# The first tokens by GpSimd's queue, the first weights on two queues: a start-up change in a gated mix of sliding attention and MLP

## The chip, the cores and the metric

One core of a Trainium2 chip runs one program. The metric is the device time in microseconds (us); lower is better. The times of the kernel before are three runs, and one further execution was profiled.

## The reference

For 2048 tokens of width 448, two branches are mixed by a gate of the token itself:

```python
g = sigmoid((x * gate_w).sum(-1, keepdims=True))
a = A(x, wqkv, wo)            # 16 heads of 28; each token attends to itself and 7 earlier ones, 2 apart
b = relu(x @ w1 + b1) ** 2 @ w2 + b2      # 448 -> 1792 -> 448
return g * a + (1 - g) * b
```

All inputs and the output are float32. In branch A, `qkv = x @ wqkv`, the eight logits of a token are scaled, masked where the position would be negative, put through a softmax, applied to the values, and multiplied by `wo`.

## The kernel before, in words

**Products in three parts.** Every operand of a matmul is kept as a high part, rounded to the chip's fp32r type, and a low part, the raw value less the high one. A product is three matmuls: high by high, high by low, low by high. So each raw tile that arrives is rounded by ScalarE (`activation(..., AF.Copy)` into an fp32r tile) and subtracted by VectorE (`tensor_sub`), and only then can all three matmuls run.

**Tiles.** The tokens are four chunks of 512, each transposed in four tiles of rows of the 448: three of 128 and one of 64, which stands twice, on both halves of the partitions. `x.h[k]` and `x.l[k]` are the high and low parts of tile k of a chunk, `x.x7` and `x.x8` those of the last. The first block of weights (queries, 448 columns and two for the gate) is `wqh`/`wql` for k = 0, 1, 2 and `w7h`/`w7l` for the last tile. Raw data land in `raws[0]` (weights, "wqraw" in the profile) and `rx` (tokens, "xraw").

**Stages.** TensorE makes q, k, v of the four chunks, which go to DRAM and come back with their halos; then attention is multiplied out on GpSimd and reduced on VectorE while TensorE does the MLP over the chunks (`ORDER`), ending with the products by `wo` and the mix.

**Order.** A planner (`Plan`) decides at build time, from costs in ns and its own clock `plan.t`, in which order jobs are put on ScalarE, VectorE, GpSimd and SyncE's DMA queue. It starts only after the opening, at `START`; the opening is written out by hand. `WARM` empty matmuls on zeros come first on TensorE (L807, "warm"). Then `qkv_first` (L429) makes the queries of chunk 0: for k = 0 it takes the first two of four token groups (columns 0 to 255, the first half) through all three products, two matmuls each, and then the other two; for k = 1 and 2 all four together. From L341 on, products run as pairs on the two halves of TensorE's rows.

**The opening's data.** ScalarE's queue brings `rx[:, 0]` in two halves of columns (L813). SyncE's queue brings the weights and the tokens of k = 1, 2 and 3 by turns (L816, L819, L821), then the other weights of chunk 0. Eight semaphores go round over the DMAs of both queues, so the ninth waits for the first to land. For k = 0, ScalarE rounds the weights (L831) and the second half of the tokens (L834), VectorE rounds the first half (L836) and makes the low parts of weights (L838) and tokens (L839). At the top, before anything else, GpSimd clears the mask (L239, L241) and a tile of zeros for the halos (L306).

Of the kernel before, what the change touches and what calls it, by code (L numbers as in the profile page):

```python
# [9 lines left out]
AF = mybir.ActivationFunctionType  # L10
# [4 lines left out]
P = 128  # L15
NS = 8
HALO = W - 1
# [6 lines left out]
NQ = D + 2  # L24
# [7 lines left out]
MM448, MM512 = 189.2, 216.0  # L32
PE_LAT = 175.0
LAT = 60.0
START = 4900.0
ORDER = (3, 0, 1, 2)
WARM = 19
FIRST = (2700.0, 2350.0, 2300.0)
PP_BUFS = 4
ST_BUFS = 3  # L40
# [143 lines left out]
def gated_mix_kernel(ctx: ExitStack, tc: tile.TileContext, xT, wqkv, w1, w2, wo, b1, b2, out):  # L184
    nc = tc.nc

    def f32(ap):
        return ap.bitcast(F32)
# [35 lines left out]
    mask = const.tile([P, NS, W], F32, name="mask")  # L224
# [11 lines left out]
    b1z = biasp.tile([P, 16], F32, name="b1z")  # L236
    b1t, none = b1z[:, :NF], b1z[0:1, 15:16]
    ctx.enter_context(tc.manual_schedule())
    nc.gpsimd.memset(mask, 0.0)  # L239
    for s in range(HALO):  # L240
        nc.gpsimd.memset(mask[0:1, s, 0:HALO - s], -1e9)  # L241

# [35 lines left out]
    def x_slot(j, o=16):  # L280
        return x_place[0][:, o + 2 * CH * j:o + 2 * CH * (j + 1)].rearrange("p (i n) -> p i n", i=2)

    def x_tiles(c):
        if c % 2:
            x_place[0] = xpool.tile([P, 8 * CH + 16], F32R, tag="x", name=f"x{c}")
            return [x_slot(j, 0 if c == 1 else 16) for j in range(4)]
        return [xap.tile([P, 2, CH], F32R, tag=f"x{j}", name=f"x{c}_{j}") for j in range(4)]
# [11 lines left out]
    wqh = ap.tile([P, 3, NP + 2 * D], F32R, name="wqh")  # L299
    wql = ap.tile([P, 3, NP + 2 * D], F32R, name="wql")  # L300
# [2 lines left out]
    ap.tile([P, 48], F32, name="pad_a")  # L303

    halo0 = smp.tile([2 * G * HALO, C], F32, tag="lg", name="halo0")
    nc.gpsimd.memset(halo0, 0.0)  # L306

    stage = {}
    stores = {(d, par): [] for d in range(3) for par in range(2)}
# [495 lines left out]

    for _ in range(WARM):
        nc.tensor.matmul(warm[:, :2 * P].rearrange("p (i n) -> p i n", i=2), zero, zeros, start=True, stop=True)  # L807

    raws = [rawp.tile([P, 4, 512], F32, tag="raw", name="wqraw0")]
    rx = rawp.tile([P, 4, 512], F32, tag="raw", name="xraw0")  # L810
    halves = slice(0, 256), slice(256, CH)
    for cols in halves:
        nc.scalar.dma_start(rx[:, 0, cols], xT[0, :, 0, cols])  # L813
    for k in range(4):
        if k < 3:
            nc.sync.dma_start(raws[0][:, k, :NQ], wqkv[0, :, k])  # L816
        else:
            for b, rows in ((0, slice(0, 64)), (1, slice(64, P))):
                nc.sync.dma_start(raws[0][rows, k, :NQ], wqkv[b, rows, k])  # L819
        if k:  # L820
            nc.sync.dma_start(rx[:, k], xT[0, :, k])  # L821
# [4 lines left out]
        raws.append(raw)  # L826
    raw7 = attp.tile([P, D], F32, tag="q", name="wqraw7")
    nc.sync.dma_start(raw7, wqkv[2, :, 3, :D])
    x = X(x_tiles(0))
    for k in range(3):  # L830
        nc.scalar.activation(wqh[:, k, :NQ], raws[0][:, k, :NQ], AF.Copy)  # L831
        for n, cols in enumerate(halves if k == 0 else (slice(0, CH),)):
            if k or n:
                nc.scalar.activation(x.h[k][:, cols], rx[:, k, cols], AF.Copy)  # L834
            else:
                nc.vector.tensor_copy(x.h[k][:, cols], rx[:, k, cols])  # L836
            if not n:
                nc.vector.tensor_sub(wql[:, k, :NQ], raws[0][:, k, :NQ], f32(wqh[:, k, :NQ]))  # L838
            nc.vector.tensor_sub(x.l[k][:, cols], rx[:, k, cols], f32(x.h[k][:, cols]))  # L839
    nc.scalar.activation(w7h[:, :NQ], raws[0][:, 3, :NQ], AF.Copy)  # L840
    nc.vector.tensor_sub(w7l[:, :NQ], raws[0][:, 3, :NQ], f32(w7h[:, :NQ]))
# [3 lines left out]

    plan.t, plan.wire = START, 15000.0
    plan.now = 9800.0
# [64 lines left out]
    for c in range(4):  # L912
        x = xs[c]
# [305 lines left out]
    rows = wo_d.rearrange("(i b) n -> i b n", b=14)  # L1219
# [31 lines left out]
    for g in range(2, 2 * NF):  # L1251
# [5 lines left out]
        if not f:  # L1257
            x, slots = X([nxt[j][0] for j in range(4)]), [nxt[j][1] for j in range(4)]
# [105 lines left out]
```

## Time and profile before

| | |
|---|---|
| timed runs, median (lowest to highest) | 393.45 us (393.07 to 393.51), 3 runs |
| the profiled execution's own time | 392.84 us |
| its span, first to last instruction | 391.1 us |
| TensorE busy in the span | 386.5 us, 99% |
| VectorE, ScalarE, GpSimd busy | 260.3, 205.4, 260.6 us |
| moved by DMA | 73.75 MB, mean 189 GB/s |

Times inside the profile count from the first instruction of the span. An engine's busy time says nothing of whether what it does is needed: the empty matmuls of the opening count as busy too. A bracket behind a row of the timeline, such as `[1.27 <-DMA wqraw<-wqkv]`, is the time for which the engine stood idle before it and what ended that. PEld is TensorE's loading of the stationary operand, which overlaps the matmul before it.

### The profile page before, as it was taken

How to read it: one execution, taken by the hardware profiler on the slowest of the kernel's cores; microseconds unless marked ns; L12 is line 12 of the kernel's file. 1: busy time of each engine (PE TensorE's matmuls, PEld its weight loads, DVE VectorE, ACT ScalarE, POOL GpSimd, SP SyncE). 2: the span in 40 equal slices, each digit the busy share in tenths (PEclk: the TensorE clock that was granted, in tenths of full speed). 3: DMA queues.
4: the chain of work that ended last, by engine and by line, in shares of the span. 5: the costliest groups of instructions: out<-in, count | busy, mean ns of one | idle time of the engine just before them, and what ended most of it. 6: DMA issues, size and time to landing. Idle time of an engine off the chain costs nothing.

```text
span 391.1 us, 9273 instructions
## 1 busy us (share of the span) xinstructions
PE 386.5 (99%) x3829; PEld 385.3 (99%) x3829; DVE 260.3 (67%) x346; ACT 205.4 (53%) x501; POOL 260.6 (67%) x165
## 2 busy tenths in 40 slices
PE   9999999999999999999999999999999999999996
PEld 8999999999999999999999999999999999999995
DVE  4525523588585778778656989789666686668454
ACT  5857865362566566445555445345716343456740
POOL 0000003979999989959999887999998979661000
PEclk9999999999999999999999999999999999999999
DMA  7999999997174062644203779645635220226835
GB/s 240 399 356 318 373 369 355 377 340 267 49 253 151 1 219 80 220 167 164 90 2 137 244 209 271 218 112 141 217 106 166 84 96 2 88 64 164 141 106 189
DMA packets 64697, 73.75 MB, mean 189 GB/s; under 512 B 32336, under 2 KB 57488, under 8 KB 64272
## 3 DMA queue, kind: packets, MB, share of 16 engines
q1 hardware_dynamic: 64224, 72.79, 56.4%
q8 instruction: 30, 0.49, 0.5%
q10 hardware_dynamic: 432, 0.38, 0.3%
q14 instruction: 11, 0.09, 0.1%
HBM read 45.71 MB, written 28.25 MB: 189 GB/s over the span
## 4 chain that ended last, share of the span: by engine, by line
PE 99%; DVE 0%; DVEq 0%; issue 0%
PE b L341 33%; PE h L341 32%; PE qkv L341 23%; PE a L341 7%; PE qkv L429 2%; PE warm L807 1%; PE a L1154 1%; DVE bt_b L1037 0%; DVEq L1359 0%
## 5 line engine op out<-in xcount | busy, mean ns | idle before, releaser
L539 POOL TENSOR_TENSOR pp<-q,k 128x896 f32<-128x896 f32 x56 | 116.8, 2119 | 75.1 <-DMA k<-k_d 63.5
L341 PE MATMUL h<-x,w1h 64*128 64x512 f32 x672 | 122.0, 376 | 0.0
L551 POOL TENSOR_TENSOR pp<-lg,v 128x896 f32<-128x896 f32 x64 | 113.9, 1868 | 9.4 <-DVE o L561 5.0
L341 PE MATMUL qkv<-wqh,x 64*128 64x448 f32 (+1 forms) x528 | 83.2, 350 | 0.0
L341 PEld LDWEIGHTS h<-x,w1h 64*128 64x128 f32 x672 | 82.8, 186 | 0.0
L341 PE MATMUL h<-x,w1l 64*128 64x512 f32 x336 | 75.9, 376 | 0.0
L793 DVE TENSOR_TENSOR h<-h,h 128x512 fp32r<-128x512 f32 x56 | 38.7, 691 | 55.1 <-ACT h L792 54.9
L543 DVE TENSOR_REDUCE lg<-pp 128x32 f32<-128x896 f32 x64 | 66.9, 1076 | 12.5 <-POOL pp L539 12.5
L341 PE MATMUL b<-w2bh,h 64*128 64x448 f32 x448 | 69.5, 349 | 0.0
L341 PE MATMUL b<-w2ah,h 64*128 64x448 f32 x448 | 69.2, 349 | 0.0
L561 DVE TENSOR_REDUCE o<-pp 128x112 f32<-128x896 f32 x64 | 67.5, 1066 | 0.0
L341 PEld LDWEIGHTS qkv<-wqh,x 64*128 64x128 f32 x528 | 61.0, 186 | 0.0
L341 PE MATMUL qkv<-wql,x 64*128 64x448 f32 (+1 forms) x264 | 56.8, 350 | 0.0
L789 ACT ACTIVATE h<-h,b1z 128x512 f32<-128x512 f32 x56 | 36.7, 655 | 37.1 <-PE h L341 37.1
L341 PEld LDWEIGHTS b<-w2bh,h 64*128 64x128 f32 x448 | 53.2, 193 | 0.0
L341 PEld LDWEIGHTS b<-w2ah,h 64*128 64x128 f32 x448 | 53.1, 193 | 0.0
L341 PE MATMUL b<-w2bl,h 64*128 64x448 f32 x224 | 47.6, 349 | 0.0
L341 PE MATMUL b<-w2al,h 64*128 64x448 f32 x224 | 47.5, 349 | 0.0
L341 PEld LDWEIGHTS h<-x,w1l 64*128 64x128 f32 x336 | 44.0, 186 | 0.0
L791 ACT ACTIVATE h<-h 128x512 fp32r<-128x512 f32 x56 | 33.4, 597 | 1.6
L363 ACT ACTIVATE st<-qkv 128x448 f32<-128x448 f32 x48 | 24.3, 539 | 17.8 <-PE qkv L341 11.5
L341 PEld LDWEIGHTS qkv<-wql,x 64*128 64x128 f32 x264 | 33.2, 186 | 0.0
(108 smaller groups left out, 576.4 us busy)
## 6 DMA issues: line engine op xcount, KB each, us to landing
v<-v_d SPq DMA_DIRECT2D x8, 840.0 KB, 6.8
x_d<-x SPq DMA_DIRECT2D x12, 512.0 KB, 7.3
x<-x_d SPq DMA_DIRECT2D x12, 512.0 KB, 4.1
k<-k_d SPq DMA_DIRECT2D x7, 840.0 KB, 7.4
q_d<-st SPq DMA_DIRECT2D x8, 448.0 KB, 5.8
k_d<-st SPq DMA_DIRECT2D x8, 448.0 KB, 5.7
v_d<-st SPq DMA_DIRECT2D x8, 448.0 KB, 6.4
o_d<-o SPq DMA_DIRECT2D x16, 224.0 KB, 2.1
```

Of the source, the lines that this page charges most:

```text
L341: nc.tensor.matmul(woven_out(acc.pt, acc.n), a[rows], woven(w[rows]), start=acc.todo == acc.all, stop=acc.todo == 1)
L363: nc.scalar.activation(st[0][:, :, t % 2].rearrange("p (i g) c -> p i g c", i=2), unwoven(pt[:, :D]).rearrange("p i (g c) -> p i g c", c=C ...
L429: nc.tensor.matmul(woven_out(acc.pt, NQ), a, woven(w), start=k == j == 0, stop=False)
L539: nc.gpsimd.tensor_mul(pr.rearrange("p (w c) -> p w c", w=W), q[:, s:s + 1].to_broadcast([P, W, C]), k[:, s:s + W])
L543: nc.vector.tensor_reduce(lgs[i][:, s], pr.rearrange("p (w h d) -> p w h d", w=W, h=HG), axis=AX.X, op=ALU.add)
L551: nc.gpsimd.tensor_mul(pr.rearrange("p (h d w) -> p w h d", h=HG, w=W), lgs[i][:, s][:, :, :, None].to_broadcast([P, W, HG, DH]), vs[i][:, ...
L561: nc.vector.tensor_reduce(o_t[par, s][:, g * C:(g + 1) * C], pr.rearrange("p (c w) -> p c w", w=W), axis=AX.X, op=ALU.add)
L789: a = add(ACT, 656.0, lambda pt=pt, r=r: nc.scalar.activation(pt, pt, AF.Relu, bias=b1t[:, f + r:f + r + 1]), ready, bias_job[0], prio=NEXT)
L791: b = add(ACT, 600.0, lambda pt=pt, hh=hh: nc.scalar.activation(hh, pt, AF.Square), a, prio=NEXT)
L793: low = add(DVE, 690.0, lambda pt=pt, hh=hh, hl=hl: nc.vector.tensor_sub(hl, pt, f32(hh)), a, prio=NEXT)
L807: nc.tensor.matmul(warm[:, :2 * P].rearrange("p (i n) -> p i n", i=2), zero, zeros, start=True, stop=True)
L1154: nc.tensor.matmul(woven_out(acc.pt, D), a, woven(w), start=False, stop=acc.todo == 1)
```

## The change

The tokens' first half of k = 0 no longer comes raw to be rounded by VectorE: GpSimd's queue brings it from DRAM straight into the fp32r tile `x.h[0][:, :256]`, with a cast on the way. The raw tile is still needed for the low part; ScalarE's queue now brings its 512 columns in one DMA. Ahead of that, the weights of k = 0 come as two DMAs of 64 rows, one on ScalarE's queue and one on SyncE's. ScalarE does a 1x1 copy into a spare place as its first operation, so that its table of functions loads there. GpSimd's memsets move behind its DMA. VectorE's rounding of the first half is gone. TensorE's empty matmuls go from 19 to 17, and the planner's start from 4900 to 4650 ns.

```diff
-START = 4900.0
+START = 4650.0
-WARM = 19
+WARM = 17
...
-    nc.gpsimd.memset(mask, 0.0)
-    for s in range(HALO):
-        nc.gpsimd.memset(mask[0:1, s, 0:HALO - s], -1e9)
...
-    nc.gpsimd.memset(halo0, 0.0)
...
     for _ in range(WARM):
         nc.tensor.matmul(warm[:, :2 * P].rearrange("p (i n) -> p i n", i=2), zero, zeros, start=True, stop=True)
 
+    x = X(x_tiles(0))
+    nc.gpsimd.dma_start(x.h[0][:, :256], xT[0, :, 0, :256])
+    nc.gpsimd.memset(mask, 0.0)
+    for s in range(HALO):
+        nc.gpsimd.memset(mask[0:1, s, 0:HALO - s], -1e9)
+    nc.gpsimd.memset(halo0, 0.0)
     raws = [rawp.tile([P, 4, 512], F32, tag="raw", name="wqraw0")]
     rx = rawp.tile([P, 4, 512], F32, tag="raw", name="xraw0")
     halves = slice(0, 256), slice(256, CH)
-    for cols in halves:
-        nc.scalar.dma_start(rx[:, 0, cols], xT[0, :, 0, cols])
+    for e, rows in ((nc.scalar, slice(64, P)), (nc.sync, slice(0, 64))):
+        e.dma_start(raws[0][rows, 0, :NQ], wqkv[0, rows, 0])
+    nc.scalar.dma_start(rx[:, 0], xT[0, :, 0])
+    nc.scalar.activation(b1z[0:1, 14:15], none, AF.Copy)
     for k in range(4):
+        if k == 0:
+            continue
         if k < 3:
             nc.sync.dma_start(raws[0][:, k, :NQ], wqkv[0, :, k])
...
-    x = X(x_tiles(0))
     for k in range(3):
         nc.scalar.activation(wqh[:, k, :NQ], raws[0][:, k, :NQ], AF.Copy)
+        nc.vector.tensor_sub(wql[:, k, :NQ], raws[0][:, k, :NQ], f32(wqh[:, k, :NQ]))
         for n, cols in enumerate(halves if k == 0 else (slice(0, CH),)):
             if k or n:
                 nc.scalar.activation(x.h[k][:, cols], rx[:, k, cols], AF.Copy)
-            else:
-                nc.vector.tensor_copy(x.h[k][:, cols], rx[:, k, cols])
-            if not n:
-                nc.vector.tensor_sub(wql[:, k, :NQ], raws[0][:, k, :NQ], f32(wqh[:, k, :NQ]))
             nc.vector.tensor_sub(x.l[k][:, cols], rx[:, k, cols], f32(x.h[k][:, cols]))
```

## The prediction

> **What bounds the kernel now.** I read the page first, for the engine that sets the end.
>
> ```profile
> span 391.1 us, 9273 instructions
> PE 386.5 (99%) x3829; PEld 385.3 (99%) x3829; DVE 260.3 (67%) x346; ACT 205.4 (53%) x501; POOL 260.6 (67%) x165
> PE 99%; DVE 0%; DVEq 0%; issue 0%
> ```
>
> Busy shares are of the span; the third line is the chain of waits by engine. TensorE (PE) is the chain. So the next question is where PE is not yet doing real work. The windows view, for PE alone (stretch, its length, PE's busy time, instructions, clock, DMA share, GB/s):
>
> ```profile
> 0.00:4.97 4.97, 4.18 (x19) 1.00 0.55 160
> 5.82:12.28 6.46, 6.46 (x36) 1.00 1.02 339
> 12.28:98.99 86.71, 86.71 (x915) 1.00 0.97 344
> 98.99:391.10 292.11, 288.28 (x2862) 1.00 0.44 139
> ```
>
> From 5.82 us PE is filled without a break; the 3.8 us missing in the last stretch are the tail behind the last matmul. Whatever moves the first matmuls moves the end by as much, and nothing that the change touches later is on the path while that filling lasts. The change can only act before about 6 us. The timeline there (start, duration, engine, line, what; in brackets the idle time before and who ended it):
>
> ```profile
> 0.74 0.90 ACTq L813 DMA_DIRECT2D xraw<-xT  x2
> 0.75 0.86 SPq L816 DMA_DIRECT2D wqraw<-wqkv  x2
> 0.79 4.39 PE L807 MATMUL warm<-const-float32-0.0 128*128 128x256 f32 x19 [0.79 <-PEq L1356]
> 1.65 0.43 SPq L821 DMA_DIRECT2D xraw<-xT  x1
> 1.67 1.28 ACT L831 ACT_TABLE_LOAD   x1 [1.67 <-PEq L1356]
> 4.22 0.58 ACT L831 ACTIVATE wqh<-wqraw 128x450 fp32r<-128x450 f32 x1 [1.27 <-DMA wqraw<-wqkv]
> 4.40 0.29 DVE L836 CAST x<-xraw 128x256 fp32r<-128x256 f32 x1 [3.54 <-DMA xraw<-xT]
> 4.55 0.33 PEld L807 LDWEIGHTS warm<-const-float32-0.0 128*128 128x128 f32 x1
> 4.84 0.63 DVE L838 TENSOR_TENSOR wql<-wqraw,wqh 128x450 fp32r<-128x450 f32 x1
> 4.86 0.45 PEld L429 LDWEIGHTS qkv<-wqh,x 128*128 128x128 f32 x2
> 4.97 0.69 PE L429 MATMUL qkv<-wqh,x 128*128 128x452 f32 x2
> 5.38 0.42 DVE L839 TENSOR_TENSOR x<-xraw,x 128x256 fp32r<-128x256 f32 x1
> 5.52 0.30 PEld L429 LDWEIGHTS qkv<-wql,x 128*128 128x128 f32 x2 [0.21 <-DVE wql L838]
> 5.52 0.65 PE L429 MATMUL qkv<-wql,x 128*128 128x452 f32 x2
> 5.55 0.42 ACT L834 ACTIVATE x<-xraw 128x256 fp32r<-128x256 f32 x1 [0.75 <-DMA xraw<-xT]
> 5.85 0.34 PEld L429 LDWEIGHTS qkv<-wqh,x 128*128 128x128 f32 x2
> 6.01 0.55 PE L429 MATMUL qkv<-wqh,x 128*128 128x452 f32 x2
> ```
>
> Read it as a ladder. The first weights land at 4.22, are rounded by 4.80, and PE loads at 4.86. The first half of the tokens lands at 4.40 and is rounded by DVE until 4.69. The warm-ups run at one per (4.55 − 0.75)/18 = 0.211 us, so the 19 of them fill PE to about 4.97, just when the first real matmul starts: nothing is lost there. Matmuls 3 and 4 (low part of the weights) are held by DVE, whose subtraction ends at 5.47: load at 5.52, and with a late load the matmul itself starts about 0.11 later, so this costs about 0.13. Matmul 5 wants the low part of the tokens' first half (DVE, 5.38 to 5.80), gets it and starts at 6.01. From then on PE steps evenly.
>
> **The change, part by part.**
>
> *Fewer warm-ups.* Two less bring the earliest start of real work from 4.97 to 4.97 − 2 × 0.211 = 4.55. This is the most that can be won in front: 0.42 us; with the 0.13 of the third matmul, 0.55 us in all, 0.14% of the time.
>
> *First weights as two halves of 64 rows, on ACT's and SP's queues.* Before, SP's queue held the weights first and ACT's the tokens, and both drained together. The DMA view of the stretch up to the weights' landing, and of the one in which ACT's queue has work (packets, MB, share of 16 engines):
>
> ```profile
> DMA packets 435, 0.58 MB, mean 137 GB/s; under 512 B 34, under 2 KB 435, under 8 KB 435
> DMA packets 648, 0.87 MB, mean 256 GB/s; under 512 B 64, under 2 KB 576, under 8 KB 648
> q1 hardware_dynamic: 360, 0.61, 58.9%
> q10 hardware_dynamic: 288, 0.26, 28.0%
> DMA packets 411, 0.70 MB, mean 377 GB/s; under 512 B 49, under 2 KB 227, under 8 KB 411
> ```
>
> The first line is 0 to 4.25 us, the next three are 1.75 to 5.15 us (q1 is SP's queue, q10 ACT's), the last 5.15 to 7 us. Until 4.25 us 0.58 MB had moved, for weights of 0.23 MB. With both queues starting on the weights, 0.23 MB, or 0.36 with all of GpSimd's half, have to move: at 0.58 MB in the 2.5 us since 1.75 that takes 1.0 to 1.6 us, and they land at 2.8 to 3.4. The rounding (0.58) then ends at about 4.0, ahead of 4.55. The weights stop being the last to come; so does their low part, at about 4.65, ahead of matmul 3. Both terms are off the path, and so the 0.13 is won.
>
> A rule of the Trainium skill speaks against this part: DMA: Bandwidth & Descriptors, section Rules for kernel authors, says of two transfers to disjoint halves of the partitions not to bother, since they share the same 16 engines. The row says that the engines are shared by what is queued first; by the rule alone the weights would still land at 4.22 (a rival below).
>
> *The table of functions.* Its load (1.67 to 2.95) already ended 1.27 us before ACT's first data. It moves nothing; the added 1x1 copy lies in the same idle time, as long as the weights land after about 3.1. Cost 0.
>
> *The tokens' first high half by GpSimd's queue, cast on the way.* DVE loses its cast of 0.29, which lay in front of the low part of the weights but ended before it could start: 0 on the path. PE now waits for the transfer itself. No row shows a transfer of this queue. Two bounds, from the page's issues to landing and from the rows of the tokens' transfers in the first 8.2 us (min/median/max):
>
> ```profile
> o_d<-o SPq DMA_DIRECT2D x16, 224.0 KB, 2.1
> DMA to landing us min/median/max: 4.3/4.7/5.5
> ```
>
> Issued at 0.75, it lands between 2.85 and 6.25; the nearest row is the same half on ACT's queue, 0.74 to 4.40. I take 4.4, just under the 4.55 at which PE is free.
>
> In a sentence apart: the skill's same page, section Latency and other measured facts, gives this queue about 1 us to the first byte against 0.6 for the others, an estimate of 0.4 us later than ACT's, so 4.8 by it.
>
> *The raw tokens, now whole, behind half the weights on ACT's queue.* This is the term that I think decides. Matmul 5 needs the low part of the first half: raw minus high. The raw first half used to land at 4.40 on its own; now it lands only with the whole 128x512, as the second thing on its queue. Before, the second half landed at 5.55. By then ACT's queue had moved 0.26 MB and SP's 0.61. Per engine, ACT's queue now has 12 packets (4 of 1.8 KB, 8 of 2.05 KB: 23.6 KB, not 16 packets with 16.4 KB). If the two queues take turns and SP's keeps its lead of some 4 packets, SP's moves 16 (29.8 KB, not 38), and GpSimd's adds 8.2 KB: 61.6 KB, not 54, or 0.12 MB in all more. At 256 GB/s that is 0.47 us, at 377 GB/s 0.32; but the engines were idle for 13.1% of those 3.4 us, 0.45 us, and a third queue may fill that, so it can be 0. If a turn costs the same with three queues as with two, 12 turns instead of 16 would even bring it 0.85 us earlier. Ends: 4.70 and 6.02. I take 5.75, between no cost and the dearer one, since part of the idle share comes before GpSimd's packets. DVE then subtracts from 5.75 to 6.17, PE loads 0.05 later and matmul 5 starts 0.11 after that, at 6.33 instead of 6.01: **+0.3 us** (+0.12 with landing at 5.55, +0.6 at 6.02). The second half's high part (ACT, 0.42) is ready at the same 6.17 for matmul 7, so it adds nothing.
>
> *Memsets behind GpSimd's transfer; the planner's start 0.25 us earlier.* The mask and the zeros for the halo are used tens of us later. The built order of PE, DVE, SP and GpSimd is otherwise the same; on ACT three weight copies (0.58 each) move behind small copies that wait for PE at about 13 and 14.6 us; the first of them is read at about 15.6, and its low part on DVE still ends more than 1 us before. Cost 0. Later transfers move by the extra 0.13 MB, 0.35 us at 377 GB/s; the tightest, the second tile's high part, has 0.3 us, and matmul 5's delay gives it as much again.
>
> **Sum.** The profiled execution took 392.84 us, 391.1 of it span; +0.3 makes 393.14. The median of the three timed runs was 393.45, 0.6 above it, so I forecast 393.45 + 0.3 = **393.75 us**. What a measurement can tell here is about 0.2%, 0.79 us.
>
> **Rivals.**
>
> 1. *The raw tokens come early and the start is won.* If they are there by 5.07, the low part is done by 5.49 and PE steps from 4.55 without a hole, matmul 5 at about 5.65 instead of 6.01: 393.45 − 0.36 = 393.1 (at best 392.9). For it: 12 turns instead of 16. Against it: more bytes ahead. Chance 0.22.
>
> 2. *Slower: GpSimd's transfer is late, and PE idles while its clock is still low.* Four matmuls stand ahead of matmul 5, so a start up to about 5.4 costs nothing beyond the 0.3; landing at 6.25 costs 0.85 more. Beside that, a load of 128 columns took 0.33 at 4.55 and about half of it from 5.52 on: PE stepped up its clock after some 4.5 us of unbroken work. If a hole from 4.55 on makes it begin that count again, up to 4.5 us more run at half speed, 2.2 us. This decides once the hole is long enough to count, which no row here shows; I put it at 0.5 us, landing after about 5. The lateness alone, in full, gives 393.75 + 0.85 = 394.6; the clock alone 393.75 + 2.2 = 396.0, half of it 394.85, which I take as the middle. For it: software makes these descriptors, and three queues share the engines. Against it: 8 packets an engine is little. Chance 0.21.
>
>    In a sentence apart: TensorE: Matmul & The Clock Gate, Part 1, has a window of about 3.4 us that must be busy, free-running; by it a broken window costs up to 1.7 us, an estimate, and the trace's 4.5 us agrees with such a window not aligned to the start.
>
> 3. *The split does nothing, as the rule on halves has it.* Then weights land at 4.22, rounding ends at 4.80, PE starts at 4.97 after 0.4 us of idling, and the third matmul's stall stays; with raw tokens as I take them matmul 5 is still at 6.33. 393.75 again, but for another reason: with early tokens 393.45. Chance 0.08.
>
> My forecast has the remaining 0.49. Its own range is 393.55 to 394.1. The stated range reaches over rival 1 below and to the middle of rival 2 above: 393.0 to 394.9; some 0.05 and 0.12 lie outside. Slower by over 0.2%, above 394.24: nearly all of rival 2 and a little of what lies above the forecast's own range, 0.24. Faster by over 0.2% means under 392.66, more than the 0.55 us that there is to win; 0.04 for what lies outside the span. Within: 0.72.
>
> **What would show it.** In the changed profile: weights' wait on ACT ends near 3.3 and not at 4.22; first real matmul at 4.55; the third not held by DVE; then a hole before matmul 5 of about 0.6 us, ended by DVE's subtraction, whose own wait was ended by the tokens' DMA at about 5.75; after it PE even, and the tail unchanged at 3.8. It is wrong if GpSimd's transfer ends the first wait, if loads stay at 0.33 beyond 5.5, if there is no hole before matmul 5, or if PE shows new idle time after 13 us.

## The result

| | before | after |
|---|---|---|
| median (lowest to highest) | 393.31 us (393.07 to 393.51), 4 runs | 396.88 us (396.57 to 398.64), 4 runs |
| the profiled execution's own time | 392.84 us | 396.67 us |
| its span | 391.1 us | 394.9 us |

The changed kernel is slower by 3.6 us: the ratio of the runs' means is 1.0100, 95% interval 1.0082 to 1.0117. The time lies above the stated range and above the highest price named in it (396.0).

### The profile page after: what moved, and what is told of

Read it like the earlier page. It is cut to its first block, busy times and chain, and to the rows that moved or that the text cites. A ratio compares the mean times of both kernels' runs of the same rounds, so it can differ in the third digit from the quotient of the medians.

```text
span 394.9 us, 9272 instructions
## 1 busy us (share of the span) xinstructions
PE 387.9 (98%) x3827; PEld 386.1 (98%) x3827; DVE 262.1 (66%) x345; ACT 205.7 (52%) x502; POOL 261.3 (66%) x166
## 4 chain that ended last, share of the span: by engine, by line
PE 97%; DMA 1%; issue 0%; DVE 0%; DVEq 0%; POOLq 0%
PE b L337 32%; PE h L337 32%; PE qkv L337 23%; PE a L337 7%; PE qkv L425 2%; DMA x<-xT 1%; PE a L1156 1%; DVE bt_b L1039 0%; DVEq L1361 0%; POOLq L1358 0%
```

## The profile after

The page's head, its chain by engine and by line and its line of GpSimd's queue; behind it the row of the waits of the first 16 us for that transfer (us in all, times, longest):

```profile
span 394.9 us, 9272 instructions
PE 97%; DMA 1%; issue 0%; DVE 0%; DVEq 0%; POOLq 0%
PE b L337 32%; PE h L337 32%; PE qkv L337 23%; PE a L337 7%; PE qkv L425 2%; DMA x<-xT 1%; PE a L1156 1%; DVE bt_b L1039 0%; DVEq L1361 0%; POOLq L1358 0%
q0 software_dynamic: 144, 0.13, 0.2%
```

```profile
PE qkv L425 <- DMA x<-xT: 2.2, 1, 2.2
```

The chain had no DMA in it; now it has one, `x<-xT`, GpSimd's transfer (q0 is its queue), and the view of waits has 2.2 us for it in one wait of PE, its longest. The timeline of the opening (the line numbers are four lower, L425 is what was L429):

```profile
0.75 0.58 SPq L815 DMA_DIRECT2D wqraw<-wqkv  x1
0.76 0.56 ACTq L815 DMA_DIRECT2D wqraw<-wqkv  x1
0.79 3.97 PE L803 MATMUL warm<-const-float32-0.0 128*128 128x256 f32 x17 [0.79 <-PEq L1358]
1.24 0.71 POOL L806 DMA_DIRECT2D x<-xT  x1 [0.78 <-POOLq L1358]
1.35 0.60 ACTq L816 DMA_DIRECT2D xraw<-xT  x1
4.06 0.58 ACT L836 ACTIVATE wqh<-wqraw 128x450 fp32r<-128x450 f32 x1 [0.58 <-DMA wqraw<-wqkv]
4.67 0.63 DVE L837 TENSOR_TENSOR wql<-wqraw,wqh 128x450 fp32r<-128x450 f32 x1 [3.80 <-ACT wqh L836]
6.99 0.62 PE L425 MATMUL qkv<-wqh,x 128*128 128x452 f32 x2 [2.23 <-DMA x<-xT]
7.31 0.42 ACT L840 ACTIVATE x<-xraw 128x256 fp32r<-128x256 f32 x1 [2.67 <-DMA xraw<-xT]
7.38 0.80 DVE L841 TENSOR_TENSOR x<-xraw,x 128x256 fp32r<-128x256 f32 x2 [2.08 <-DMA xraw<-xT]
7.86 0.96 PEld L425 LDWEIGHTS qkv<-wqh,x 128*128 128x128 f32 x4 [0.22 <-DVE x L841]
```

The weights come 0.16 us earlier than before (4.06 against 4.22) and are ready, high part and low, by 5.30. PE has had its last warm-up at 4.76 and stands still for 2.23 us, until the tokens' first half has come by GpSimd's queue. The raw tokens, needed for the low part, come only at 7.3, so the fifth matmul waits another 0.22. The first real matmul moves from 4.97 to 6.99: 2.0 of the 3.8 us. The rest is in the windows of PE:

```profile
4.76:6.99 2.23, 0.00 (x0) 1.00 1.02 231
6.99:8.20 1.21, 1.21 (x6) 1.00 1.01 370
8.20:11.62 3.42, 3.42 (x11) 0.50 1.07 314
11.62:15.92 4.30, 4.30 (x25) 1.00 1.07 398
15.92:102.63 86.71, 86.71 (x915) 1.00 0.96 335
102.63:394.90 292.27, 288.28 (x2863) 1.00 0.45 139
```

The fourth column is the granted clock. It is full for the first six matmuls (6.99 to 8.20), but from 8.20 on PE works for 3.42 us at half of it, with 11 matmuls where 25 fit into the next 4.30. That is 3.42 × 0.5 = 1.71 us. The last two rows have the same 86.71 and nearly the same last stretch as before (292.11), 3.64 us later: 2.02 in the start, and 1.62 between the first real matmul and the long stretch (6.99 to 15.92, before 4.97 to 12.28), which is the clock's 1.71 with small differences both ways. So nearly everything is lost in the first 12 us. The rest of the 3.8 is 0.16 in the tail, where the last output takes that much longer from its issue to the end of the span.

One more pair of rows shows how the opening's transfers fared as a whole, 3 to 5 us, first of the kernel before, then of the changed one:

```profile
DMA packets 456, 0.58 MB, mean 290 GB/s; under 512 B 57, under 2 KB 413, under 8 KB 456
```

```profile
DMA packets 188, 0.27 MB, mean 137 GB/s; under 512 B 8, under 2 KB 104, under 8 KB 188
q1 hardware_dynamic: 11, 0.01, 1.5%
```

Just where the first data should land, less than half as much moves, and SP's queue (q1) next to nothing.

## The experiments

My theory, from this trace: GpSimd's transfer lands too late (6.9), PE idles, and the idle time brings the clock down. Rivals: the split of the weights is part of the loss; the cast is what makes the transfer late; the small things (warm-ups, table, memsets) matter. The ratios are to the kernel before on the same chip, whose medians were 393.0 to 394.0 us.

**The clock alone, from both sides.** First, the changed kernel with enough warm-ups that PE never idles; second, the kernel before with so few that it idles for 2 us and nothing else is changed.

```diff
 # e1_covered, from the changed kernel
-WARM = 17
+WARM = 30
 # e6_hole, from the kernel before
-WARM = 19
+WARM = 9
```

> The changed kernel with 30 empty matmuls instead of 17, so that TensorE has no hole between them and its first real matmul (6.99 us in the changed kernel; 30 at 0.213 us last until about 7.2). Theory, lateness and clock as two separate prices: the granted clock, 0.5 from 8.20 to 11.62 us in the changed kernel, stays at 1.0 there; the start is as late as before, so the time is about 393.3 + 7.2 - 4.97 = 395.4 to 395.6 us, 1.3 to 1.5 better than the changed kernel's 396.9. Rival, the clock is no price of its own (it falls back whatever TensorE does, or costs nothing): 396.9 to 397.1 us, with the same 3.41 us at 0.5. Third: if the transfer itself is later by chance, the first real matmul shows it.

> The kernel before with 9 empty matmuls instead of 19: TensorE stands idle from about 2.7 us to 4.86 us and nothing else changes. Theory, a hole of about 2 us costs by itself, through the clock: the first real matmul stays at 4.97, the granted clock stays 0.5 for one more stretch of 3.41 us (to about 8.6 us), 1.0 to 1.7 us more: 394.3 to 395.1 us. Rival, the hole costs nothing: 393.3 us and the clock at 1.0 from 5.2 us on.

e1_covered: 395.88 us (395.28 to 396.45), ratio 1.0065 (1.0050 to 1.0081); the median lies 0.3 above what I expected. With the clock at full from the first real matmul on, 0.9 us of the 3.6 is gone by the medians, 1.4 by the ratios. (A weight load of its empty matmuls still takes 0.33 us at 6.0 us and 0.19 at 6.8. So in this execution the clock opened only shortly before the real work: the empty matmuls brought it up rather than kept it up.) It is not the whole 1.71, since the first real matmul comes 0.15 later and PE at full clock runs into the next late tile: its timeline shows a wait of 0.39 for ScalarE, which had got the second tile's tokens only at 9.38.

```profile
7.14 0.62 PE L425 MATMUL qkv<-wqh,x 128*128 128x452 f32 x2
10.06 1.03 PE L425 MATMUL qkv<-wqh,x 128*128 128x452 f32 x4 [0.39 <-ACT x L840]
```

e6_hole: 394.66 us (394.14 to 395.72), ratio 1.0039 (1.0021 to 1.0058): the first real matmul comes at 5.05, as it does before within 0.1 us, and the hole ahead of it alone costs 1.5 us. The profiled execution took 395.72 us, 1.1 above the median, so it shows more of the effect. Its timeline, and two of PE's windows:

```profile
5.05 1.12 PE L429 MATMUL qkv<-wqh,x 128*128 128x452 f32 x2 [2.01 <-ACT wqh L831]
```

```profile
9.00:10.00 1.00, 1.00 (x4) 1.00 0.95 330
11.00:12.00 1.00, 1.00 (x7) 1.00 1.05 393
```

Four matmuls a us at 9 us, seven at 11. (The clock column says 1.00 in both; a low clock at the very start is not in it, so the counts have to be read.) So e1 and e6 show the second half of rival 2: an idle PE of 2 us in the opening is paid twice, once as waiting and once in the clock.

**Without GpSimd's transfer.** The tokens' first half comes raw on ScalarE's queue again and VectorE rounds it; the split of the weights, the early table, 17 warm-ups stay.

```diff
-    nc.gpsimd.dma_start(x.h[0][:, :256], xT[0, :, 0, :256])
...
-    nc.scalar.dma_start(rx[:, 0], xT[0, :, 0])
+    for cols in halves:
+        nc.scalar.dma_start(rx[:, 0, cols], xT[0, :, 0, cols])
...
+    nc.vector.tensor_copy(x.h[0][:, :256], rx[:, 0, :256])
```

> The changed kernel without GpSimd's transfer: the raw tokens come in two halves on ScalarE's queue behind its half of the weights, and VectorE rounds the first half as in the kernel before; split weights, early table, 17 empty matmuls and the planner's start stay. Theory, all of the loss comes from GpSimd's transfer: the tokens' first half lands near 4.4 us, first real matmul between 4.55 and 5.1, time 393.0 to 393.6 us, within 0.2% of before. Rival, the split of the weights (or the ninth DMA's wait) is part of the loss: SyncE's first packet stays late (2.48 us, 1.76 before), tokens land past 5 us, 394 us or more; if then the hole is long the granted clock falls back too and it is 395 to 396.5.

394.89 us (394.03 to 396.09), ratio 1.0044 (1.0027 to 1.0062): my expectation missed, the rival held. About half of the loss is gone, the other half stays without any transfer by GpSimd. Its timeline says why, with a window of PE behind it, and the DMA view of 3.25 to 5 us beside it:

```profile
4.12 0.58 ACT L837 ACTIVATE wqh<-wqraw 128x450 fp32r<-128x450 f32 x1 [0.17 <-DMA wqraw<-wqkv]
5.73 0.29 DVE L835 CAST x<-xraw 128x256 fp32r<-128x256 f32 x1 [4.87 <-DMA xraw<-xT]
6.17 0.62 PE L425 MATMUL qkv<-wqh,x 128*128 128x452 f32 x2 [1.42 <-DVE x L835]
9.00:10.00 1.00, 1.00 (x7) 1.00 1.06 278
```

```profile
DMA packets 183, 0.23 MB, mean 131 GB/s; under 512 B 17, under 2 KB 181, under 8 KB 183
```

The weights gain 0.1 us, and the tokens behind half of them on ScalarE's queue come at 5.73 instead of 4.40. PE idles for 1.42 us, and in this execution (394.25 us) that is not paid again in the clock: seven matmuls a us behind it, as in e6 at 11 us.

**Does the cast make it late?** The same transfer without a cast, into a spare raw tile; VectorE rounds from there.

```diff
-    nc.gpsimd.dma_start(x.h[0][:, :256], xT[0, :, 0, :256])
+    xg = early[:, 0, 0, :256]
+    nc.gpsimd.dma_start(xg, xT[0, :, 0, :256])
...
+        if k == 0:
+            nc.vector.tensor_copy(x.h[0][:, :256], xg)
```

> The changed kernel with GpSimd's transfer taking the same 128x256 without a cast, into a spare raw tile; VectorE rounds it from there (0.29 us more before the first matmul). Queues, bytes and order are the same. Theory, the cast in the transfer makes it slow: it lands by about 4.5 us, the first real matmul stands near 5 us and the time is 393.5 to 394.2 us. Rival, the software queue (or three queues together) is slow with or without a cast: lands near 6.9 us, first real matmul near 7.3, the clock falls back, 396.8 to 397.4 us.

397.87 us (2 runs), ratio 1.0116 (1.0095 to 1.0137). It lands at 7.1. The cast is not the cause.

```profile
7.13 0.29 DVE L840 CAST x<-early 128x256 fp32r<-128x256 f32 x1 [1.91 <-DMA early<-xT]
```

**Is it the 64 rows?** As e2_no_gpsimd, but the weights are cut by columns, 128 rows each.

```diff
-    for e, rows in ((nc.scalar, slice(64, P)), (nc.sync, slice(0, 64))):
-        e.dma_start(raws[0][rows, 0, :NQ], wqkv[0, rows, 0])
+    for e, cols in ((nc.scalar, slice(224, NQ)), (nc.sync, slice(0, 224))):
+        e.dma_start(raws[0][:, 0, cols], wqkv[0, :, 0, cols])
```

> As the run without GpSimd's transfer, but the first weights are split between ScalarE's and SyncE's queue by columns (128 rows of 226 and of 224) and not by rows (64 rows of 450); the same bytes, the same order, 17 empty matmuls. In the run without GpSimd's transfer, issues of 64 rows took 0.56 to 0.59 us and those behind them up to 0.82, SyncE's first packet came at 2.48 us and not 1.76, and from 4.0 to 4.75 us hardly a packet moved. Theory, transfers of 64 rows make that: here issues take about 0.4, SyncE's first packet comes near 1.8, no gap in the packets, weights land near 3.3, the tokens' first half by 4.5, first real matmul at 4.55 to 4.9: 392.8 to 393.3 us. Rival, it is the two queues opening together on one tile, or the order, whatever the shape: first packet near 2.5, the gap stays, 394.5 to 395.2 us.

395.03 us (393.90 to 396.27), ratio 1.0047 (1.0030 to 1.0063). That theory fell: the weights do come sooner, and the time is that of e2.

```profile
3.56 0.56 ACT L837 ACTIVATE wqh<-wqraw 128x450 fp32r<-128x450 f32 x1
5.56 0.29 DVE L835 CAST x<-xraw 128x256 fp32r<-128x256 f32 x1 [4.70 <-DMA xraw<-xT]
6.00 0.62 PE L425 MATMUL qkv<-wqh,x 128*128 128x452 f32 x2 [1.69 <-DVE x L835]
```

What is lost here is not the shape of the weights but the place of the tokens behind them. In the landings of the sixteen DMA engines, 14 have brought their share of the tokens' first half by 4.8 us, and the last two at 5.1 and 5.5: who waits for a transfer waits for its slowest engine. And the 64 rows by themselves, in the kernel before with the early table: both on SP's queue, with the tokens left alone on ScalarE's:

```diff
-        if k < 3:
+        if k == 0:
+            for rows in (slice(0, 64), slice(64, P)):
+                nc.sync.dma_start(raws[0][rows, 0, :NQ], wqkv[0, rows, 0])
+        elif k < 3:
```

> The kernel before with one thing changed in its transfers: SyncE's first weights go out as two transfers of 64 rows, one behind the other on its own queue (with ScalarE's 1x1 copy ahead, so that the table does not wait for the weights). ScalarE's queue brings the tokens' halves as before. Theory, the shape of 64 rows is enough: its issues take about 0.56, the packets of the following transfers come with a gap between 3 and 5 us, the tokens' first half or the first weights land past 4.8, 393.8 to 395 us. Rival, the split over two queues is what does it: lands as before within 0.3 us, 393.1 to 393.5 us.

394.11 us (393.79 to 395.55), ratio 1.0028 (1.0017 to 1.0040). Each of the two issues takes SP's queue 0.6 us, the second half of the weights lands at 5.5, and the tokens' half at 4.0: what stands second on its queue comes late. The time is in the range of the theory. Whether the 64 rows or the cut into two transfers on one queue costs it is open, since no run puts two cuts by columns on one queue.

```profile
5.55 0.58 ACT L835 ACTIVATE wqh<-wqraw 128x450 fp32r<-128x450 f32 x1 [2.42 <-DMA wqraw<-wqkv]
```

**GpSimd's transfer without the split.** Whole weights on SP's queue, 19 warm-ups, the planner's 4900, no early table; the transfer, the whole raw tokens and the memsets behind the transfer stay.

```diff
-WARM = 17
+WARM = 19
...
-    for e, rows in ((nc.scalar, slice(64, P)), (nc.sync, slice(0, 64))):
-        e.dma_start(raws[0][rows, 0, :NQ], wqkv[0, rows, 0])
+    nc.sync.dma_start(raws[0][:, 0, :NQ], wqkv[0, :, 0])
```

> GpSimd's transfer alone: the changed kernel with the first weights whole on SyncE's queue as in the kernel before, 19 empty matmuls, the planner's start at 4900 and no early table; GpSimd's queue brings the cast half, ScalarE's queue the whole raw tokens. Theory now, the slump in the packets comes from the transfers of 64 rows and GpSimd's transfer was a victim of it: it lands by 4.9 us, and only the whole raw tokens make matmul 5 late by 0.3 us or less: 393.2 to 394.0 us. Rival, GpSimd's transfer has a price of its own: it lands near 6 us or later, the clock falls back and it is 395 to 396.5 us.

397.41 us (396.68 to 399.09), ratio 1.0111 (1.0090 to 1.0132): the split had not made the transfer late, as I had thought. The profiled execution took 399.09 us, 1.7 above the median; in it the clock is at half from 7.8 to 13.87 us, longer than in the changed kernel. Its timeline, and the row of the transfer's issue with the us from issue to landing at its end:

```profile
7.83 0.72 PE L425 MATMUL qkv<-wqh,x 128*128 128x452 f32 x1 [3.33 <-DMA x<-xT]
```

```profile
x<-xT POOLq DMA_DIRECT2D x1, 128.0 KB, 6.5
```

**All but these two.** The kernel before with 17 warm-ups, the planner's 4650 and the early table.

> The rest of the change alone: the kernel before with 17 empty matmuls, the planner's start at 4650 and the early table, and with none of the moved transfers. Theory, none of these is part of the loss: the data land as before, a hole of 0.4 us opens before the first real matmul at 4.9 to 5.0, the clock opens as before: 393.1 to 393.5 us. Rival, a hole of 0.4 us is enough to hold the clock back, or the early table delays ScalarE: 394 us or more.

393.13 us (392.92 to 395.59), ratio 1.0007 (0.9994 to 1.0021). Nothing. So the loss lies in the moved transfers, and they make a table (its lower row has the raw tokens whole besides, in one transfer):

| | weights whole on SP's queue | weights on two queues, tokens behind |
|---|---|---|
| tokens' half raw, by ScalarE's queue | 393.13 (e10), ratio 1.0007 | 394.89 (e2), ratio 1.0044 |
| tokens' half by GpSimd's queue, raw tokens whole | 397.41 (e8), ratio 1.0111 | 396.88 (changed), ratio 1.0100 |

They don't add. In the timelines both make PE wait for the same half of the tokens, so that the later one counts; the table agrees with that and doesn't prove it.

**Does the transfer hurt where nobody waits for it?** The kernel before with the same transfer into a spare buffer, and the memsets behind it.

```diff
+    nc.gpsimd.dma_start(w2al[:, 0, :256], xT[0, :, 0, :256])
```

> The kernel before with one transfer more: GpSimd's queue brings the same 128x256 of tokens with the cast at the same place as in the changed kernel, but into a spare place that nobody waits for. Weights and token halves go as before. Theory, GpSimd's transfer is late by itself (with the weights whole it landed at 7.70 us, with a first packet at 4.28) and does little to the other queues: it lands past 5.5 us here too, the first real matmul stays within 0.2 us of 4.97, 393.1 to 393.5 us. Rival, it takes the engines from the other two queues: their first transfers, 4.2 and 4.4 us before, land past 4.8, the first matmul past 5.3, 393.6 to 395 us.

394.53 us (394.01 to 394.59), ratio 1.0031 (1.0020 to 1.0043). The rival held in the time: it costs 1.5 us by the medians as a bystander, 1.2 by the ratio. The first landings moved by less than it said. In the timeline the weights and the tokens come 0.36 and 0.35 later than before, at 4.58 and 4.75, and the second half of the tokens 1.08 later. This half, and the second tile, which comes at 8.28, hold PE for 0.19 and 0.45:

```profile
4.58 0.58 ACT L832 ACTIVATE wqh<-wqraw 128x450 fp32r<-128x450 f32 x1 [1.63 <-DMA wqraw<-wqkv]
6.63 0.42 ACT L835 ACTIVATE x<-xraw 128x256 fp32r<-128x256 f32 x1 [1.47 <-DMA xraw<-xT]
7.10 0.65 PE L425 MATMUL qkv<-wqh,x 128*128 128x452 f32 x2 [0.19 <-ACT x L835]
8.96 1.03 PE L425 MATMUL qkv<-wqh,x 128*128 128x452 f32 x4 [0.45 <-ACT x L835]
```

**The whole raw tokens alone.** This was the term that I had called the deciding one.

```diff
-    for cols in halves:
-        nc.scalar.dma_start(rx[:, 0, cols], xT[0, :, 0, cols])
+    nc.scalar.dma_start(rx[:, 0], xT[0, :, 0])
```

> The kernel before with the first tokens brought raw in one transfer of 512 columns on ScalarE's queue, not two of 256; VectorE rounds the first half when all of it is there. This measures the term that the prediction took to decide, on a queue where it stands first. Theory, whole it lands when the second half did, 5.3 to 5.6 us: first matmul at about 5.8 and, with a hole of 0.8 us, 394.0 to 394.4 us, more where the clock falls back. Rival, one transfer of larger packets is as fast as the first half was: 4.6 to 4.9 us and 393.2 to 393.6 us.

393.92 us (393.57 to 395.63), ratio 1.0022 (1.0013 to 1.0032): +0.9. It lands by 5.13, first on its queue, and pushes the weights back as well (4.95 against 4.22).

```profile
4.95 0.58 ACT L830 ACTIVATE wqh<-wqraw 128x450 fp32r<-128x450 f32 x1 [2.48 <-DMA wqraw<-wqkv]
5.13 0.29 DVE L835 CAST x<-xraw 128x256 fp32r<-128x256 f32 x1 [4.27 <-DMA xraw<-xT]
```

**Why is GpSimd's transfer late?** Four runs asked that. In e11_two_queues, ScalarE's queue is empty and SP's brings weights, raw tokens and all else; in e14_memsets_first, from the changed kernel, GpSimd's memsets go ahead of its transfer again; in e15_quiet, from e11, SP's later loads wait until the first weights are rounded; in e13_calm, the kernel before has one more transfer of 128 KB by GpSimd, without a cast, at about 355 us.

```diff
 # e11_two_queues (against e8_gpsimd_alone)
-    nc.scalar.dma_start(rx[:, 0], xT[0, :, 0])
+    nc.sync.dma_start(rx[:, 0], xT[0, :, 0])
 # e15_quiet (against e11_two_queues), ahead of the other loads
+    nc.scalar.activation(wqh[:, 0, :NQ], raws[0][:, 0, :NQ], AF.Copy)
+    nc.scalar.activation(raws[0][0:1, 1, 0:1], none, AF.Copy)
 # e13_calm (against the kernel before), at the end
+    nc.gpsimd.dma_start(smp.tile([P, 256], F32, tag="lg", name="calm"), xT[0, :, 0, :256])
```

> As the run with GpSimd's transfer alone, but the whole raw tokens go on SyncE's queue behind the first weights, so that ScalarE's queue is empty and GpSimd's has one other beside it. Theory, GpSimd's transfer is late because its descriptors come late and slowly, whoever else is there: its first packet again more than 1.5 us after its issue began and the last landing past 5.5 us; 395 to 397.5 us. Rival, three queues at once are what slows it: it lands by 4.9 us, the first matmul near 5, and 393.3 to 394.3 us.

> The kernel before, and one more transfer on GpSimd's queue: the same 128 KB (128 rows of 256 columns, no cast) as the change brings at the start, but here issued at the very end of GpSimd's work, near 350 us, into a buffer that nobody reads. The question is whether it is this queue that needs 5.6 to 6.5 us from issue to landing wherever it is used, or the start of the program that makes it so. Theory (it is the start, where both other queues are filled with megabytes and the machinery wakes up): here it lands 2 to 3.5 us after its issue, first packet within 1.5 us. Rival (the queue is as slow as that by itself): 5 us or more from issue to landing here too. The time should be that of the kernel before, 393.2 +- 0.5, either way, since nobody waits for it before the end of the program.

> The changed kernel with GpSimd's memsets back ahead of its transfer; all else as changed. What may delay the transfer's packets on GpSimd itself: its memsets (1.95 to 2.61) run just while its descriptors would be written. Theory A (the memsets behind it hold the transfer up): first packet under 1 us after the end of its issue, landing before 6 us, time 395.5 or less. Theory B (they have nothing to do with it): the transfer is issued some 0.2 to 0.6 us later, and lands at 6.5 to 7.8 us as it did before; time 396.5 to 397.8.

> Of the version with whole weights and whole raw tokens on SP's queue and nothing on ScalarE's: now every later load on SP's queue waits until ScalarE has rounded the first weights (near 4 us), so that in the first 4 us only 0.49 MB stand before the engines, GpSimd's 0.13 MB among 0.62 in all. The later tiles come late, so the time says nothing; what counts is when GpSimd's transfer starts and lands. Theory A (it is late because megabytes of the other queue stand before the engines at the start): first packet by 3.3 us and landing by 5.5 us, 4.3 after its issue or less. Theory B (it is late by itself, some 5 us from issue to landing, and slow packets at 3 to 5 us belong to the start and not to the load): first packet at 4 us or later, landing at 6 us or later.

e11: 397.66 us (396.60 to 397.87), ratio 1.0107 (1.0093 to 1.0121); e14: 398.04 us (2 runs), ratio 1.0107 (1.0045 to 1.0169); e13: 393.67 us (393.19 to 393.96), ratio 1.0001 (0.9990 to 1.0012); e15: 395.72 us, one run. The rows of the transfer's issue, with the us to landing at the end: e11, e14, e13, e15 with PE's first real matmul behind it, and last the changed kernel:

```profile
x<-xT POOLq DMA_DIRECT2D x1, 128.0 KB, 6.5
```

```profile
x<-xT POOLq DMA_DIRECT2D x1, 128.0 KB, 6.4
```

```profile
calm<-xT POOLq DMA_DIRECT2D x1, 128.0 KB, 4.8
```

```profile
x<-xT POOLq DMA_DIRECT2D x1, 128.0 KB, 4.7
```

```profile
6.05 0.62 PE L425 MATMUL qkv<-wqh,x 128*128 128x452 f32 x2 [1.04 <-DMA x<-xT]
```

```profile
x<-xT POOLq DMA_DIRECT2D x1, 128.0 KB, 5.6
```

Neither ScalarE's queue (e11) nor the memsets (e14) have to do with it. Where little else is queued (e15) it needs 4.7 us, and 4.8 in the middle of the program (e13): between what my two theories had said there, nearer to the one by which this queue is slow by itself. What the load of the other queues adds at the start is 0.9 (changed) to 1.8 us (e11). With an issue at 1.24, the 4.7 alone make a landing at 5.9, and PE is free at 4.76: in none of these versions does the transfer come in time.

Not settled is why the other queues' packets become slow while this transfer is pending. In e11, from 3 to 4.25 us, no packet of GpSimd's queue has run yet and SP's queue works alone:

```profile
DMA packets 67, 0.12 MB, mean 97 GB/s; under 512 B 8, under 2 KB 8, under 8 KB 67
q1 hardware_dynamic: 67, 0.12, 63.0%
```

63% of the engines' time for 97 GB/s, where the kernel before moves 290 in 94% of it (3 to 5 us): half as much for the same busy time. But e2 has a slack stretch too, 131 GB/s in 62% of the time, without any transfer by GpSimd, so the pending transfer isn't the only thing that slows them.

No version that was run beats the kernel before; e10 is level with it.

## Why the prediction was wrong

By its own steps:

- *Fewer warm-ups: right as far as it went.* PE was free at 4.76 and would have started; there was nothing to start with.
- *The split brings the weights at 2.8 to 3.4: mis-sized, and its price left out.* Their wait ended at 4.06, not near 3.3; the gain is 0.16 us. The sum "0.58 MB in 2.5 us" took the rate of the kernel before for granted, but in 3 to 5 us 137 GB/s were moved, not 290. The rule of the Trainium skill that I had set against this part (DMA: Bandwidth & Descriptors, Rules for kernel authors: two transfers to disjoint halves share the same engines, don't bother) agrees with 4.06 against 4.22. Cut by columns, which the rule does not speak of, the weights did come by 3.56 (e5), near the forecast, and the time was no better. What the prediction did not price at all is the queue place: the tokens that had ScalarE's queue to themselves now stand behind weights. e2 and e5 measure that at 1.7 to 1.9 us.
- *"I take 4.4" for GpSimd's transfer: the step that failed.* It landed at 6.9, beyond even the upper bound of 6.25, so a term that the sum had at 0 on the path became the 2.23 us for which PE waits; the first wait ended by this transfer is a sign of being wrong that I had named. I had priced a queue that no row showed by the row of another queue, because it was the same data. The rows for the bounds were those of the other two queues as well, so the upper end was too low too. And I had let it be issued at 0.75, like theirs; it was issued at 1.24. The Trainium skill's about 1 us to the first byte (DMA: Bandwidth & Descriptors, Latency and other measured facts) is not borne out either. In e15, with little else queued, the first packet ran at 3.53, 2.3 us after the issue began and 1.6 after it ended, and the landing came at 5.9, 4.7 us after it began; the estimate by the page had been 4.8.
- *The raw tokens as the deciding term: real, but not the one that decided.* I took 5.75, between 4.70 and 6.02, and the raw tokens came at 7.3, so this term was mis-sized by more than its bounds allowed. With the high half there in time and nothing else moved, matmul 5 would have stood near 7.8 for it; no run shows the two apart in this way. Alone on its queue it costs 0.9 us (e12), and in the changed kernel it adds only the 0.22 before the fifth matmul, since PE starts at 6.99 and the raw tokens come at 7.3. The forecast of a hole ended by VectorE's subtraction, behind the tokens' DMA, was right in form; it was 0.22 and not 0.6, at 7.86 and not at 6.33.
- *Rival 2 was the case, and its two prices were to be added.* I had 0.85 for the lateness and 2.2 for the clock, and named each alone (394.6 and 396.0) with a middle of 394.85. Measured are 2.02 and 1.71 in the profile. A late transfer that makes the hole makes both at once; together they would have been 393.75 + 0.85 + 2.2 = 396.8, beside a median of 396.88, though with both terms off. That they come so near the median is luck. The range ended at the middle of that rival, and 0.21 was little for a queue that no row had shown.
- *The clock: the fall was right, its course was not.* "If a hole makes it begin that count again" would have put PE at half clock right behind the hole. The windows show it at full clock for the first six matmuls (6.99 to 8.20), and only then at half. The half-clock stretch lasts 3.42 us, where I had allowed 4.5; here the row agrees with the page TensorE: Matmul & The Clock Gate, Part 1, of the Trainium skill, which has a free-running window of about 3.4 us. But its advice (Why this matters for your kernels: no idle gaps over some 3 us) is too lenient for this case: a gap of 2.23 us was enough, and one of 2.01 kept the clock low in e6. Gaps of 1.42 (e2) and 1.69 us (e5) did not bring it down in the profiled executions (seven matmuls in the us from 9 to 10 in both), and one of 0.2 us, as in e10, cost nothing.
- *Table, memsets, planner at 0: right*, table and planner by e10; for the memsets, e14's two runs show no gain from their old place. Third matmul no longer held by VectorE, no new wait after 13 us: right, and worth nothing here, since the first wait is longer than all of them. The tail is 0.16 us longer.

## What to carry to other kernels

A transfer on a queue that the trace has never shown is an unknown with no upper row: run it by itself first, or take a range that includes twice the nearest row. In an opening, ask what stands behind what on each queue before asking how fast it moves: the start waits for the slowest engine of the last tile, and putting anything ahead of a tile costs that tile. And a long hole in TensorE's work (2.0 to 2.2 us here, not yet 1.7) is priced as waiting plus clock; warm-ups that reach over a late arrival win back part of it.

## What the runs showed of the hardware that was not expected

- A transfer of 128 KB by GpSimd's queue takes 4.7 to 4.8 us from issue to landing with little beside it (e15, e13), and 5.6 to 6.5 at the start beside the others; a cast makes no difference that these runs can show (5.9 without it).
- It costs the other queues up to 1.08 us on their own landings, though it is 0.13 MB (e9).
- A 64-row transfer holds its queue for 0.56 to 0.6 us at issue, where one of 128 rows in the same place took 0.39 (e8, e11).
- An idle gap of 2.0 to 2.2 us in TensorE's work in the opening costs 0.9 to 1.4 us (e1) and 1.5 us (e6) in the clock alone, while gaps of 1.42 (e2) and 1.69 us (e5) left it at full in the profiled executions.
